# Grouping score and dP chunks by four, with remainder channels at four row positions and the softmax row-sum correction moved out of dS

## The chip, the cores and the metric

The kernel runs on one core of one Trainium2 chip. The metric is the device time of one execution in microseconds (us), as the median of several runs. A core has five engines that run side by side and synchronise by semaphores: PE (matrix multiplies, with PEld for its weight loads), DVE (vector work), ACT (activations, copies with a scale), POOL (general work on the on-chip memory SBUF) and SP (here only a queue that issues transfers). Matmul results go to PSUM, eight banks of accumulation memory, from which DVE and ACT read.

## The reference, cut to what matters

The kernel computes the output and all gradients of one block. B = 2 batches, T = 4000 tokens, D = 144 channels, everything in bfloat16.

```python
xa = _layernorm(x)
qkv = jnp.einsum('btd,de->bte', xa, w_qkv)
scores = jnp.einsum('btd,bsd->bts', q, k) * D ** (-0.5)
p = _softmax(scores, axis=-1)
attn = jnp.einsum('bts,bsd->btd', p, v)
glob = jnp.einsum('btd,de->bte', attn, w_att_out)
...
h = _gelu(jnp.einsum('btd,de->bte', xc, w_mlp_in))
...
m = jnp.concatenate([glob, loc], axis=-1)
...
return x + jnp.einsum('btc,cd->btd', m, w_merge)
...
_out, _vjp = jax.vjp(_f, x, w_qkv, w_att_out, w_mlp_in, dw_csgu, w_mlp_out, dw_merge, w_merge)
_grads = _vjp(grad_out)
```

The part that matters here is attention, forwards and backwards. Per query row the kernel needs P = exp(S - max) unnormalised, its row sum l, Y = P xa / l, then dP (the gradient that reaches P), delta = the row's dot product of Y with dP's own query-side factor, and dS = P (dP - delta) / l. From dS come Z = dS xa (the gradient on the query side) and X, the sum over query rows of dS and P times query-side factors (the gradient on the key and value side).

## The kernel before

The 4000 tokens of a batch are 32 tiles (NB) of 125 tokens (PB). The channels are 128 main ones and 16 remainder ones (DR): `xaT_m` holds the transposed main channels, `R` holds in rows 0 to 15 the remainder channels and in rows 16 to 111 a stack of gradient remainders for other products. Keys are cut into 8 chunks (NG) of 500 (CH).

Each batch runs `phase_att`, then a merge phase; a final phase follows the second batch. `phase_att` is a software pipeline over steps t = 0 to 32. Within a step t the slots s = 0 to 7 hold:

- s = 0 to 3: `S_pair(t, s)`, scores of tile t against two chunks. For each chunk one matmul over the main channels (L683) and one over `R` (L684, 128 rows high, with zero weights beyond the 16). One `ps` tile (two PSUM banks, two such tiles exist in `ps_sg`) takes both chunks. DVE copies the negative to `Pbuf` while it takes the running minimum (L688, L690), ACT writes the exponential over it (L691).
- s = 0: transposes of Z of tile t-3. s = 1: `jit_mm(t + 1)`, the query-side factors `qb`. s = 4: `jit_tr(t + 1)`, their transposes `qt`, the weights of the score and dP matmuls.
- s = 2, 3: `Y_half(t - 1, ...)`, 32 matmuls of 145 columns over the transposed P (`PT`), then on DVE the reciprocal `rl` of the row sum (column 144) and `delta`; on ACT the stored `yn` and `QBs`, both query-side factors times `rl` in one instruction (L725). s = 3 ends with `rescale(t)`, which brings the four quarters of P to one maximum and issues the transposing transfer to `PT` (L703).
- s = 4 to 7: `dP_pair(t - 1, ...)`, which mirrors `S_pair` (L733, L734). DVE makes `Sbuf` = (dP - delta) P from it, one instruction for each chunk (L739).
- s = 6, 7: `Z_half(t - 2, ...)`, 32 matmuls of 144 columns over the transposed dS (`ST`), then ACT's scaled copy `zn`.
- `x(n)`: groups of `X_group`, which multiply `Sbuf` and `Pbuf` blocks of tiles t-3 and t-2 with `QBs` (L794), and DVE's sum into `acc` (L800).
- `local(...)`: units of the other branch of the block (convolution, GELU and their gradients), spread over the steps.

At the end of a step the transposing transfer from `Sbuf` to `ST` is issued (L859). After the loop `last_tr` transposes the last tile's dS on PE, into `PT`, which is free then; the last Z and X follow, mixed with matmuls of the merge phase (`M.fill`). Transfers are issued in order on SP's queue: `Yn_d`, `Zn_d`, `PT`, `ST` and `ug_d`, each behind the one before it. The order on each engine is that of the text, changed in places by a scheduler that orders ready work.

## Time and profile before

| what | us |
|---|---|
| median of 3 runs (lowest to highest) | 1480.2 (1479.16 to 1481.11) |
| the profiled execution, its time | 1477.11 |
| its span, first to last instruction | 1475.3 |
| busy: PE | 1377.6 |
| busy: DVE | 1217.1 |
| busy: ACT | 849.7 |
| busy: POOL | 282.0 |

The profile records one execution. Busy time of an engine is the union of its instructions' times. A line of a group names the source line, engine, operation, the tile written and those read, the shape, how often it occurs, its busy time and the mean ns of one, and the idle time of the engine just before. A duration of PE contains the draining of the array, so that neighbours overlap; the distance between starts says what one costs. The two attention loops lie from 59 to about 655 us and from 770 to about 1365 us of the span.

### The profile page before, as it was taken

How to read it: one execution, taken by the hardware profiler on the slowest of the kernel's cores; microseconds unless marked ns; L12 is line 12 of the kernel's file. 1: busy time of each engine (PE TensorE's matmuls, PEld its weight loads, DVE VectorE, ACT ScalarE, POOL GpSimd, SP SyncE). 2: the span in 40 equal slices, each digit the busy share in tenths (PEclk: the TensorE clock that was granted, in tenths of full speed). 3: DMA queues.
4: the chain of work that ended last, by engine and by line, in shares of the span. 5: the costliest groups of instructions: out<-in, count | busy, mean ns of one | idle time of the engine just before them, and what ended most of it. 6: DMA issues, size and time to landing. Idle time of an engine off the chain costs nothing. (4 is left out here: it accounts for less than half of the span.)

```text
span 1475.3 us, 39163 instructions
## 1 busy us (share of the span) xinstructions
PE 1377.6 (93%) x16184; PEld 1181.5 (80%) x16184; DVE 1217.1 (82%) x3060; ACT 849.7 (58%) x1538; POOL 282.0 (19%) x494
## 2 busy tenths in 40 slices
PE   2789999999999999997888999999999999999898
PEld 1568888888888888887885888888888888888797
DVE  6699888988898988887638998889898889888754
...
GB/s 101 31 144 121 121 121 122 120 122 117 118 115 113 119 118 111 107 138 209 62 56 104 138 122 113 111 121 124 119 123 121 121 121 121 116 117 124 218 35 64
DMA packets 559360, 170.44 MB, mean 116 GB/s; under 512 B 542443, under 2 KB 554093, under 8 KB 559136
## 3 DMA queue, kind: packets, MB, share of 16 engines
...
## 5 line engine op out<-in xcount | busy, mean ns | idle before, releaser
L739 DVE SCALAR_TENSOR_TENSOR Sbuf<-ps,delta,Pbuf 125x500 bf16<-125x500 f32 x512 | 356.0, 731 | 28.2 <-PE ps L734 25.4
L794 PE MATMUL X<-QBs,Sbuf 125*125 125x144 bf16 x2048 | 303.1, 226 | 6.7 <-DVE acc L800 3.0
L794 PE MATMUL X<-QBs,Pbuf 125*125 125x144 bf16 x2048 | 302.1, 226 | 0.0
L794 PEld LDWEIGHTS <-Pbuf 125*125 125x125 bf16 x2048 | 262.1, 137 | 14.9 <-issue 10.3
L794 PEld LDWEIGHTS <-Sbuf 125*125 125x125 bf16 x2048 | 261.9, 137 | 7.7 <-DVE Sbuf L739 2.0
L800 DVE TENSOR_TENSOR acc<-X,acc 125x432 f32<-125x432 f32 x372 | 203.4, 550 | 33.0 <-PE X L794 31.9
L683 PE MATMUL ps<-xaT_m,qt 128*125 128x500 bf16 x512 | 194.6, 380 | 11.2 <-ACT Pbuf L691 9.9
L733 PE MATMUL ps<-xaT_m,qt 128*125 128x500 bf16 x512 | 192.7, 376 | 8.0 <-ACT Pbuf L691 5.7
L684 PE MATMUL ps<-R,qt 128*125 128x500 bf16 x512 | 194.0, 379 | 0.0
L734 PE MATMUL ps<-R,qt 128*125 128x500 bf16 x512 | 191.2, 373 | 0.0
L711 PEld LDWEIGHTS <-PT 125*125 125x125 bf16 x2048 | 147.9, 137 | 24.3 <-DMA PT<-Pbuf 6.5
L755 PEld LDWEIGHTS <-ST 125*125 125x125 bf16 x1984 | 144.2, 138 | 18.1 <-DMA ST<-Sbuf 0.6
L711 PE MATMUL yz<-xa_aug,PT 125*125 125x145 bf16 x2048 | 151.1, 227 | 4.1 <-DMA PT<-Pbuf 4.0
L755 PE MATMUL yz<-xa_aug,ST 125*125 125x144 bf16 x1984 | 147.8, 228 | 0.4 <-DMA ST<-Sbuf 0.4
L684 PEld LDWEIGHTS <-qt 128*125 128x125 bf16 x512 | 70.8, 138 | 33.3 <-issue 14.2
L734 PEld LDWEIGHTS <-qt 128*125 128x125 bf16 x512 | 69.8, 136 | 27.7 <-issue 8.2
L547 POOL TENSOR_TENSOR A_dwc<-l_fl,A_dwc 128x512 f32<-128x512 f32 (+2 forms) x48 | 35.7, 744 | 292.8 <-ACT l_fl L546 292.8
L688 DVE TENSOR_SCALAR_CACHE_REDUCE Pbuf<-ps 125x1000 bf16<-125x1000 f32 x64 | 76.6, 1197 | 14.5 <-PE ps L684 14.3
L733 PEld LDWEIGHTS <-qt 128*125 128x125 bf16 x512 | 70.0, 137 | 23.1 <-DVE Sbuf L739 2.7
L683 PEld LDWEIGHTS <-qt 128*125 128x125 bf16 x512 | 70.6, 138 | 21.9 <-issue 1.3
L759 ACT ACTIVATE zn<-yz,rl 125x144 bf16<-125x144 f32 x64 | 24.2, 378 | 108.5 <-PE yz L755 108.5
L417 POOL TENSOR_SCALAR l_a<-l_sq 125x576 bf16<-125x576 bf16 x32 | 21.4, 670 | 292.6 <-ACT l_sq L415 252.9
...
## 6 DMA issues: line engine op xcount, KB each, us to landing
...
PT<-Pbuf SPq DMA_TRANSPOSE x64
```

The source lines that it names most:

```text
L547: nc.gpsimd.tensor_tensor(acc, fl[0:rows, 0:n], acc, op=ALU.add)
L683: nc.tensor.matmul(ps[:, h, 0:CH], qt[:, 0, :], xaTm[:, cs], start=True, stop=False)
L684: nc.tensor.matmul(ps[:, h, 0:CH], qt[:, 1, :], R[:, cs], start=False, stop=True)
L688: nc.vector.tensor_scalar(pdst, src, -1.0, None, op0=ALU.mult, op1=ALU.min, accum_out=nm[:, 0:1])
L711: nc.tensor.matmul(Y, PT[0:PB, j, 0:PB], xaa[:, j, 0:D + 1], start=(j == 0), stop=(j == NB - 1))
L733: nc.tensor.matmul(ps[:, h, 0:CH], qt[:, 2, :], xaTm[:, cs], start=True, stop=False)
L734: nc.tensor.matmul(ps[:, h, 0:CH], qt[:, 3, :], R[:, cs], start=False, stop=True)
L739: nc.vector.scalar_tensor_tensor(sdst, ps[:, h, 0:CH].rearrange("p (a b) -> p a b", b=PB), DL[i][:], psrc, op0=ALU.subtract, op1=ALU.mult)
L755: nc.tensor.matmul(Z, ST[0:PB, j, 0:PB], xaa[:, j, 0:D], start=(j == 0), stop=(j == NB - 1))
L759: nc.scalar.activation(zn[:, 0:D], Z, ACT.Copy, scale=RL.pop(i)[:])
L794: nc.tensor.matmul(X[:, jj, :], l, r, start=(n_ == 0), stop=(n_ == len(ops) - 1))
L800: nc.vector.tensor_tensor(av, X[:, 0:nj, :], av, op=ALU.add)
```

## The change

- `quad` takes four pieces of work and gives each its own bank: four main matmuls (L684 of the new file), then four remainder matmuls of 16 rows (L688) that are kept behind the last main one. The r-th remainder stands at rows 32r to 32r+15.
- For that, `XR` holds the 16 remainder rows at four row positions, copied out of `R` by four transfers for each two chunks; in `qb` POOL copies the remainder channels to three more places, so that the transposed `qt` has them at the four row positions.
- In a step with both tiles, `products(c2)` groups two score chunks of tile t and two dP chunks of tile t-1. Such a group takes both `ps` tiles.
- `PdP` makes `Sbuf` = dP P, without delta, one DVE instruction for both chunks. The term delta P is put elsewhere: Z gets `ty`, which is -delta / l times Y's unnormalised sum, added (`zs` on ACT, the sum on POOL), and the factor that X multiplies with `Pbuf` gets -delta times the other query-side factor (`nd` and `gq` on POOL). `QBs` is written by two ACT instructions.
- `Y_half(t - 1)` moves to the step's end, `Z_half(t - 2)` behind the second group; the transfer to `ST` is cut in two, the first half behind the second group, the second at the step's end, ahead of `rescale(t)`.
- Behind the loop `last_tr` writes to `ST`; the last tile's Y stands there too, with `late_y` behind it.

```diff
@@ -346,6 +346,10 @@
             for bi in range(8):
                 nc.tensor.transpose(pr[0:DR, bi, 0:PB], S.xa_aug[:, 8 * g + bi, 128:D], W.ident[0:PB, 0:PB])
             nc.vector.tensor_copy(v8(S.R, 8 * g, 8)[0:DR], pr[0:DR, :, 0:PB])
+
+            for r in range(4):
+                c = 2 * g + r % 2
+                nc.sync.dma_start(S.XR[32 * r:32 * r + DR, g, :], S.R[0:DR, c * CH:(c + 1) * CH])
 
         def go_rem():
             nc.gpsimd.tensor_copy(S.go_r[:], go_q[:, :, 128:D])
@@ -641,8 +645,8 @@
             nc.gpsimd.memset(t_[:, :, D:256], 0.0)
         for t_ in znr:
             nc.gpsimd.memset(t_[:, D:256], 0.0)
-        xaTm, R, xaa = S.xaT_m, S.R, S.xa_aug
-        QT, QB, RL, DL, YZ, ZN, ZT, NM, DHT = {}, {}, {}, {}, {}, {}, {}, {}, {}
+        xaTm, R, XR, xaa = S.xaT_m, S.R, S.XR, S.xa_aug
+        QT, QB, RL, TY, YZ, ZN, ZT, NM, DHT = {}, {}, {}, {}, {}, {}, {}, {}, {}
         units = local_units(k, W, b, S, A, es_loc, DHT, ps_w)
 
         def jit_mm(i):
@@ -655,6 +659,8 @@
                 nc.tensor.matmul(pj[:, D:2 * D], S.goT[:, h * PB:(h + 1) * PB], W.VUT[:, kk, 0:D], start=False, stop=(kk == 4))
             qb = qbr[i % 3]
             nc.scalar.copy(qb[:, :, 0:D], pj[:].rearrange("p (a b) -> p a b", b=D))
+            rem_ = qb[:, :, 128:256].rearrange("p a (r c) -> p a r c", c=32)[:, :, :, 0:DR]
+            nc.gpsimd.tensor_copy(rem_[:, :, 1:4, :], rem_[:, :, 0:1, :].to_broadcast([PB, 2, 3, DR]))
             QB[i] = qb
 
         def jit_tr(i):
@@ -670,25 +676,42 @@
         def pchunk(pb, c2):
             return Pbuf[0:PB, pb, c2 * 1024:(c2 + 1) * 1024]
 
-        def S_pair(i, c2):
-            qt = QT[i]
+        def quad(work):
+
+
+            pp = [ps_sg.tile([PB, 2, 512], F32, tag="sg", name="ps") for _ in range(len(work) // 2)]
+            for r, (qt, q, c) in enumerate(work):
+                mm = nc.tensor.matmul(pp[r // 2][:, r % 2, 0:CH], qt[:, q, :], xaTm[:, c * CH:(c + 1) * CH], start=True, stop=False)
+            with tc.issue_after(mm.ins), tc.high_priority():
+                for r, (qt, q, c) in enumerate(work):
+                    rs = slice(32 * r, 32 * r + DR)
+                    nc.tensor.matmul(pp[r // 2][:, r % 2, 0:CH], qt[rs, q + 1, :], XR[rs, c // 2, :], start=False, stop=True)
+            return [p[:, :, 0:CH].rearrange("p h (a b) -> p h a b", b=PB) for p in pp]
+
+        def S_work(i, c2):
+            return [(QT[i], 0, 2 * c2), (QT[i], 0, 2 * c2 + 1)]
+
+        def dP_work(i, c2):
+            return [(QT[i], 2, 2 * c2), (QT[i], 2, 2 * c2 + 1)]
+
+        def pv(buf, n, c2):
+            return buf[0:PB, n, c2 * 1024:(c2 + 1) * 1024].rearrange("p (h a b) -> p h a b", h=2, b=128)[:, :, :, 0:PB]
+
+        def S_exp(i, c2, src):
             if c2 == 0:
                 nm_ = small.tile([PB, 8], F32, tag="nm")
                 NM[i] = nm_
             nm = NM[i]
-            ps = ps_sg.tile([PB, 2, 512], F32, tag="sg")
-            for h in range(2):
-                c = 2 * c2 + h
-                cs = slice(c * CH, (c + 1) * CH)
-                nc.tensor.matmul(ps[:, h, 0:CH], qt[:, 0, :], xaTm[:, cs], start=True, stop=False)
-                nc.tensor.matmul(ps[:, h, 0:CH], qt[:, 1, :], R[:, cs], start=False, stop=True)
-            src = ps[:, :, 0:CH].rearrange("p h (a b) -> p h a b", b=PB)
-            pdst = pchunk(i % NPB, c2).rearrange("p (h a b) -> p h a b", h=2, b=128)[:, :, :, 0:PB]
+            pdst = pv(Pbuf, i % NPB, c2)
             if c2 == 0:
                 nc.vector.tensor_scalar(pdst, src, -1.0, None, op0=ALU.mult, op1=ALU.min, accum_out=nm[:, 0:1])
             else:
                 nc.vector.tensor_scalar(pdst, src, -1.0, nm[:, c2 - 1:c2], op0=ALU.mult, op1=ALU.min, accum_out=nm[:, c2:c2 + 1])
             nc.scalar.activation(pdst, src, ACT.Exp, bias=nm[:, c2:c2 + 1], scale=1.0)
+
+        def PdP(i, c2, src):
+
+            nc.vector.tensor_tensor(pv(Sbuf, i % NDB, c2), src, pv(Pbuf, i % NPB, c2), op=ALU.mult)
 
         def rescale(i):
             nm = NM.pop(i)
@@ -703,7 +726,7 @@
             nc.sync.dma_start_transpose(out=PT[:], in_=Pbuf[:, i % NPB, :])
 
         def Y_half(i, h):
-            if h == 0:
+            if h == 0 and i not in YZ:
                 yz = ps_yz.tile([PB, 2, 145], F32, tag="yz")
                 YZ[i] = yz
             Y = YZ[i][:, 0, :]
@@ -716,27 +739,22 @@
             RL[i] = rl
             nc.vector.reciprocal(rl[:], Y[:, 144:145])
             delta = small.tile([PB, 1], F32, tag="delta")
-            DL[i] = delta
             dj = small.tile([PB, D], BF, tag="dj", bufs=1)
             nc.vector.scalar_tensor_tensor(dj[:], Y[:, 0:D], rl[:], qb[:, 1, 0:D], op0=ALU.mult, op1=ALU.mult, accum_out=delta[:])
             yn = small.tile([PB, D], BF, tag="yn", bufs=2)
             nc.scalar.activation(yn[:], Y[:, 0:D], ACT.Copy, scale=rl[:])
             nc.sync.dma_start(S.Yn_d[:, i, :], yn[:])
-            nc.scalar.activation(QBs[:, i % NPB], qb[:, :, 0:D], ACT.Copy, scale=rl[:])
-
-        def dP_pair(i, c2):
-            qt = QT[i]
-            ps = ps_sg.tile([PB, 2, 512], F32, tag="sg")
-            for h in range(2):
-                c = 2 * c2 + h
-                cs = slice(c * CH, (c + 1) * CH)
-                nc.tensor.matmul(ps[:, h, 0:CH], qt[:, 2, :], xaTm[:, cs], start=True, stop=False)
-                nc.tensor.matmul(ps[:, h, 0:CH], qt[:, 3, :], R[:, cs], start=False, stop=True)
-            for h in range(2):
-                c = 2 * c2 + h
-                psrc = Pbuf[0:PB, i % NPB, c * 512:(c + 1) * 512].rearrange("p (a b) -> p a b", b=128)[:, :, 0:PB]
-                sdst = Sbuf[0:PB, i % NDB, c * 512:(c + 1) * 512].rearrange("p (a b) -> p a b", b=128)[:, :, 0:PB]
-                nc.vector.scalar_tensor_tensor(sdst, ps[:, h, 0:CH].rearrange("p (a b) -> p a b", b=PB), DL[i][:], psrc, op0=ALU.subtract, op1=ALU.mult)
+            nd = small.tile([PB, 2], F32, tag="nd")
+            nc.gpsimd.tensor_scalar(nd[:, 0:1], delta[:], -1.0, None, op0=ALU.mult)
+            nc.gpsimd.tensor_tensor(nd[:, 1:2], nd[:, 0:1], rl[:], op=ALU.mult)
+            gq = small.tile([PB, D], F32, tag="gq", bufs=1)
+            nc.gpsimd.tensor_scalar(gq[:], qb[:, 0, 0:D], nd[:, 0:1], None, op0=ALU.mult)
+            nc.gpsimd.tensor_tensor(gq[:], gq[:], qb[:, 1, 0:D], op=ALU.add)
+            ty = small.tile([PB, D], F32, tag="ty", bufs=2)
+            nc.scalar.activation(ty[:], Y[:, 0:D], ACT.Copy, scale=nd[:, 1:2])
+            TY[i] = ty
+            nc.scalar.activation(QBs[:, i % NPB, 0, :], qb[:, 0, 0:D], ACT.Copy, scale=rl[:])
+            nc.scalar.activation(QBs[:, i % NPB, 1, :], gq[:], ACT.Copy, scale=rl[:])
 
         def last_tr(c2):
 
@@ -744,9 +762,9 @@
             sb = Sbuf[0:PB, (NB - 1) % NDB, c2 * 1024:(c2 + 1) * 1024].rearrange("p (a b) -> p a b", b=128)
             for j in range(8):
                 nc.tensor.transpose(pt[0:PB, j, 0:PB], sb[:, j, 0:PB], W.ident[0:PB, 0:PB])
-            (nc.vector.tensor_copy if c2 % 2 else nc.scalar.copy)(PT[0:PB, 8 * c2:8 * c2 + 8, 0:PB], pt[0:PB, :, 0:PB])
-
-        def Z_half(i, h, ST=ST):
+            (nc.vector.tensor_copy if c2 % 2 else nc.scalar.copy)(ST[0:PB, 8 * c2:8 * c2 + 8, 0:PB], pt[0:PB, :, 0:PB])
+
+        def Z_half(i, h):
             if h == 0 and i + 1 not in YZ:
                 yz = ps_yz.tile([PB, 2, 145], F32, tag="yz")
                 YZ[i + 1] = yz
@@ -756,7 +774,9 @@
             if h == 0:
                 return
             zn = znr[i % 2]
-            nc.scalar.activation(zn[:, 0:D], Z, ACT.Copy, scale=RL.pop(i)[:])
+            zs = small.tile([PB, D], F32, tag="zs", bufs=1)
+            nc.scalar.activation(zs[:], Z, ACT.Copy, scale=RL.pop(i)[:])
+            nc.gpsimd.tensor_tensor(zn[:, 0:D], zs[:], TY.pop(i)[:], op=ALU.add)
             nc.sync.dma_start(S.Zn_d[:, i, :], zn[:, 0:D])
             ZN[i] = zn
 
@@ -823,40 +843,51 @@
                 for _ in range(n):
                     if xg:
                         X_group(*xg.pop(0))
-            for s in range(8):
-                if s < 4 and ok(t):
-                    S_pair(t, s)
-                if s >= 4 and ok(t - 1):
-                    dP_pair(t - 1, s - 4)
-                if t == NB and s == 4:
-                    M.late_y()
-                if s == 0:
-                    if ok(t - 3):
-                        zt_tr(t - 3)
-                    x(1)
-                elif s == 1:
-                    if ok(t + 1):
-                        jit_mm(t + 1)
-                    x(1)
-                elif s in (2, 3):
+            def loc(f):
+                local(-(-int(n_units * (t + f) * 1000) // (1000 * (NB - 1))))
+
+            def products(c2):
+                if t < NB:
+                    ps = quad((S_work(t, c2) if ok(t) else []) + (dP_work(t - 1, c2) if ok(t - 1) else []))
+                    S_exp(t, c2, ps[0])
                     if ok(t - 1):
-                        Y_half(t - 1, s - 2)
-                    if s == 3 and ok(t):
-                        rescale(t)
-                elif s == 4:
-                    if ok(t + 1):
-                        jit_tr(t + 1)
-                    x(1)
-                elif s == 5:
-                    x(1)
-                else:
-                    if ok(t - 2) and t < NB:
-                        Z_half(t - 2, s - 6)
-                    x(1)
-                local(-(-n_units * (8 * t + s + 1) // (8 * (NB - 1))))
+                        PdP(t - 1, c2, ps[1])
+                elif c2 < 2:
+                    for q, src in enumerate(quad(dP_work(t - 1, 2 * c2) + dP_work(t - 1, 2 * c2 + 1))):
+                        PdP(t - 1, 2 * c2 + q, src)
+            products(0)
+            if ok(t - 3):
+                zt_tr(t - 3)
+            loc(0.25)
+            if ok(t + 1):
+                jit_mm(t + 1)
+            loc(0.5)
+            x(1)
+            products(1)
+            for h in range(2):
+                if ok(t - 2):
+                    Z_half(t - 2, h)
+            if ok(t - 1) and t < NB:
+                nc.sync.dma_start_transpose(out=ST[:, 0:NB // 2, :], in_=Sbuf[:, (t - 1) % NDB, 0:GW // 2])
+            x(1)
+            loc(0.6)
+            products(2)
+            if ok(t + 1):
+                jit_tr(t + 1)
+            x(1)
+            loc(0.95)
+            x(1)
+            products(3)
+            if t < NB:
+                for h in range(2):
+                    if ok(t - 1):
+                        Y_half(t - 1, h)
+            loc(1.0)
             x(6)
-            if t < NB and ok(t - 1):
-                nc.sync.dma_start_transpose(out=ST[:], in_=Sbuf[:, (t - 1) % NDB, :])
+            if t < NB:
+                if ok(t - 1):
+                    nc.sync.dma_start_transpose(out=ST[:, NB // 2:NB, :], in_=Sbuf[:, (t - 1) % NDB, GW // 2:GW])
+                rescale(t)
             if t == NB - 1:
                 M.open_early(ST)
         es_sg.close()
@@ -865,17 +896,17 @@
         xg = X_groups(NB + 1)
         for c2 in range(4):
             last_tr(c2)
+        zt_tr(NB - 2)
+        for h in range(2):
+            Y_half(NB - 1, h)
+        M.late_y()
+        M.fill(2)
+        for h in range(2):
+            Z_half(NB - 1, h)
+        for _ in range(5):
             X_group(*xg.pop(0))
-        Z_half(NB - 2, 0)
-        Z_half(NB - 2, 1)
+        M.fill(4)
         X_group(*xg.pop(0))
-        M.fill(2)
-        Z_half(NB - 1, 0, PT)
-        Z_half(NB - 1, 1, PT)
-        zt_tr(NB - 2)
-        M.fill(2)
-        X_group(*xg.pop(0))
-        M.fill(2)
         zt_tr(NB - 1)
         for g_ in X_groups(NB + 2):
             X_group(*g_)
@@ -1291,6 +1322,7 @@
     bx = pool(ctx, "bx", "left")
     xaT_m = bx.tile([128, T], BF, name="xaT_m")
     R = bx.tile([128, T], BF, name="R")
+    XR = bx.tile([128, G8, CH], BF, name="XR")
     go_r = bx.tile([PB, NB + 6, DR], BF, name="go_r")
     goT = bx.tile([128, (NB + 4) * PB], BF, name="goT")
     acc = bx.tile([PB, NB, D], F32, name="acc")
@@ -1300,7 +1332,7 @@
     SS = [K() for _ in range(B)]
     SS[0].xa_aug = px0.tile([PB, NB, XW], BF, name="xa_aug0")
     for b, S in enumerate(SS):
-        S.xaT_m, S.R, S.go_r, S.goT, S.acc, S.rstd_x = xaT_m, R, go_r, goT, acc, rstd[b]
+        S.xaT_m, S.R, S.XR, S.go_r, S.goT, S.acc, S.rstd_x = xaT_m, R, XR, go_r, goT, acc, rstd[b]
         for nm in ("Yn", "ug", "Zn"):
             setattr(S, nm + "_d", tc.dram_tile([PB, NB, D], BF, name="%s_d%d" % (nm, b)))
     A = K()
```

## The prediction

> **What bounds the kernel now.** I read the page's totals first, then its groups.
>
> ```profile
> PE 1377.6 (93%) x16184; PEld 1181.5 (80%) x16184; DVE 1217.1 (82%) x3060; ACT 849.7 (58%) x1538; POOL 282.0 (19%) x494
> ...
> L739 DVE SCALAR_TENSOR_TENSOR Sbuf<-ps,delta,Pbuf 125x500 bf16<-125x500 f32 x512 | 356.0, 731 | 28.2 <-PE ps L734 25.4
> ...
> L684 PE MATMUL ps<-R,qt 128*125 128x500 bf16 x512 | 194.0, 379 | 0.0
> ...
> L688 DVE TENSOR_SCALAR_CACHE_REDUCE Pbuf<-ps 125x1000 bf16<-125x1000 f32 x64 | 76.6, 1197 | 14.5 <-PE ps L684 14.3
> ```
>
> PE leads, with DVE not far behind. An average hides stages, so next comes a stretch of 24 whole steps of the first attention loop, cut at first score matmuls.
>
> ```profile
> core 0: us, PE busy (x) PEld busy (x) DVE busy (x) ACT busy (x) POOL busy (x), PEclk, DMA share, GB/s
> 137.57:592.45 454.88, 446.49 (x5188) 382.08 (x5187) 403.42 (x939) 283.02 (x510) 53.36 (x84) 1.00 0.66 118
> ```
>
> Divided by 24, a step takes 18.95 us: PE is busy 18.60, DVE 16.81, ACT 11.79, POOL 2.22, at a full clock. PE sets the step and idles 0.35 us of it. The second loop's stretch has the same 446.5 in 454.7. What a matmul costs is not its 380 ns (they overlap) but the distance to the next start, from PE's order of time:
>
> ```profile
> 306.95 0.37 PE L683 MATMUL ps<-xaT_m,qt 128*125 128x500 bf16 x1
> 307.16 0.37 PE L684 MATMUL ps<-R,qt 128*125 128x500 bf16 x1
> 307.37 0.37 PE L683 MATMUL ps<-xaT_m,qt 128*125 128x500 bf16 x1
> 307.58 0.37 PE L684 MATMUL ps<-R,qt 128*125 128x500 bf16 x1
> 307.79 0.27 PE L767 MATMUL pt<-ident,zn 125*128 125x125 bf16 x2
> ```
>
> Four take 0.84 us: 211 ns each, and the remainder (L684, 16 useful rows) as much as the main part. Eight such pairs make 6.75 us of a step. Matmuls of 144 columns, Y, Z and X, follow each other at 63 ns (twelve of X from 307.90 to 308.66).
>
> **What PE saves.** The change replaces, per four chunks, eight full-height matmuls (8 x 211 = 1688 ns) by four mains (844) and four 16-row remainders at four row positions. No row of this trace shows matmuls side by side at different row positions. If all four run together they cost one, 211 ns; if none do, 844. Between stands the weight load: loads of 125 columns follow each other at 58 ns in the stream of L514 (five in 0.45 us, each 0.22 long), so I let the four start 58 ns apart: 211 + 3 x 58 = 385. The nearest end is the lower one, since each has its own weights, rows and bank; I do not take it because every remainder still needs its load.
>
> Changing between 128 and 16 rows is in the trace, in the preparation:
>
> ```profile
> 41.46 0.22 PE L231 MATMUL pt<-ident,Wi 128*96 128x128 bf16 x1
> 41.61 0.20 PE L232 MATMUL pt<-ident,Wi 16*96 16x16 bf16 x1
> 41.75 0.26 PE L231 MATMUL pt<-ident,Wi 128*96 128x128 bf16 x1
> 41.93 0.20 PE L232 MATMUL pt<-ident,Wi 16*96 16x16 bf16 x1
> 42.07 0.26 PE L231 MATMUL pt<-ident,Wi 128*96 128x128 bf16 x1
> ```
>
> There and back takes 0.32 us (41.75 to 42.07). Streaming explains 55 ns for 128 columns (L480) and at most as much for 16, so the two changes cost 210 to 265 ns. Changing to 80 rows (L1054) shows no such pause; if this one belonged to the transposes alone the price would be zero. Same rows, same engine: I take 250 ns for the there and back of a group.
>
> A group then costs 844 + 385 + 250 = 1479 ns and saves 209; four groups save 0.84 us a step. The ends: 844 + 211 + 0 = 1055 saves 2.53 us a step, and 844 + 844 + 265 = 1953 loses 1.06.
>
> The Trainium skill, "TensorE: Matmul & The Clock Gate", section "Part 3: Packing small matmuls — row/col tiling", gives 3.07x for four row tiles of 512 columns. By that figure an estimate of the remainders is 844 / 3.07 = 275 ns, a group 1369, and the total below would come to 1404; no row here shows it.
>
> **What the other engines get.** DVE: eight STTs of 731 ns become four tensor-tensor products over 1000 elements. L800 takes 298 ns for 144 and 600 for 432 elements, 1.05 ns an element: 1196 for 1000, as L688's 1197. DVE falls by 5.85 - 4.78 = 1.06 us to 15.75 a step; not counted in the sum, since PE stays above it.
>
> ACT: one 288-column scaling of 532 (L725) becomes two of about 378 (L759's size), and ty adds one: 0.6 us, to 12.4. POOL: six small operations a step. By L547's 80x144 sum (485), L338 (561 upper, 471 lower for L338's first batch), L459 (272) and L925 (180) they are 2 x 180 + 470 + 2 x 485 + 272 = 2.1 us, to 4.3 of 18. Neither engine is near the step. In the loops DVE's L739 takes 731 ns on average where POOL is idle (398 cases) and 735 where POOL works beside it (54), so more POOL work costs DVE nothing.
>
> The added wait is on ACT: ty waits for nd, the second QBs scaling for gq, both on POOL. Behind them stand the rescale and the next step's first exponential. Y's end, reciprocal 0.17, dot 0.45, POOL 1.3, hops 0.4, scalings 0.4: 2.7 us, then rescale 1.4. The next first exponential is wanted after 21 matmuls of X (1.3), a group (1.5) and the minimum (1.3): 4.1. It fits exactly. A 1.29 us POOL sum (L547) in between makes it late by that much, and PE's next group late with it; that falls in about one step of four, 0.1 us a step on the sum below as a cost.
>
> SP: the transfer of ST is cut in two; a whole one occupies the queue as follows.
>
> ```profile
> L859 SPq DMA_TRANSPOSE ST<-Sbuf x62: 4764/4855/6453, 87.3 to 1362.3; - x62
> ```
>
> The second half, behind yn's store, is issued about 1.2 us after Y's end and (half of 4.9, plus half of the whole's 5 us of traffic, partly overlapped) is there about 5 us after it. Z's second half starts 7.6 us after (X 1.3, group 1.5, fill 2.5, group 1.5, first Z half 1.0, less the overlap). 2 us of cover; PT has a whole step. If the cover went, PE would wait and DVE after it. The 16 XR copies per batch are 0.25 us each on SP, behind R's copies and past the stores of the merge; only a step's last group needs the last of them. I take 0.5 us a batch (0 to 3).
>
> **Score buffers.** A group takes both ps buffers, where a pair took one. The next group waits for minimum, exponential and product.
>
> ```profile
> 308.40 1.19 DVE L688 TENSOR_SCALAR_CACHE_REDUCE Pbuf<-ps 125x1000 bf16<-125x1000 f32 x1
> ...
> 309.63 1.10 ACT L691 ACTIVATE Pbuf<-ps,nm__4762 125x1000 bf16<-125x1000 f32 x1 [1.17 <-DVE Pbuf L688]
> ```
>
> That is 1.2 to 1.3 + 1.1 + hops: 2.6 us. PE's other work of a step, 18.60 - 6.75 = 11.85 us, lies in four stretches: by the order of the program, about 2.5 (jit, local), 3.0 (Z and X), 2.6 and 3.6 (Y and X). So the wait is just covered if DVE starts the minimum at once; DVE's work per stretch is about 4.3, 3.2, 4.3 and 4.6 us against PE's 4.0, 4.5, 4.1 and 5.1, so it catches up. I raise idle time from 0.35 to 0.45 us, the 0.1 from ACT's wait.
>
> **The sum.** A step: 18.60 - 0.84 + 0.45 = 18.21, 0.74 less than 18.95; 62 steps (31 a loop) give -46. Half groups at each loop's first step cost 4 x 2 x 0.1 = +0.8. The tail, with Y of the last tile behind the transposes, is between -2 and +4 a batch, +1 taken, since POOL's loads have 19 us between Yn's store (656) and its reading (682); XR +1. The profiled execution took 1477.1 us by its timing (span 1475.3 and 1.8 around it): 1477.1 - 46 + 4 = 1435. The median of the runs, 1480.2, lies 3 above: 1438.
>
> **Rivals.**
>
> Remainders start together and the change of rows costs its least: group 844 + 211 + 210 = 1265, saving 1.69 us a step, PE at 16.9, DVE at 15.75 next to bind; with 0.4 idle, 17.3 a step, -102: 1382. For it: nothing in the four shares rows or a bank; against: the loads. With free changes of rows PE and DVE meet near 16 and it reaches 1335.
>
> The wait for both buffers decides (slower): DVE is 87% busy, and an X sum of 0.6 us (L800) queued before a minimum delays the buffers by that. The forecast's margin is 0.74 us a step, 0.19 a group; above that the kernel is slower. With half the groups delayed 0.6 and 0.05 of hops, 0.35 a group or 1.4 a step: +0.66 x 62 = +41, 1521. For it: before, the wait of DVE's minimum for PE was 51.9 us in 70 cases (the list of waits) and PE's for the exponential 9.9 in 13, with a spare buffer, now gone; against: the stretches above. The Trainium skill, "TensorEngine Tiling (Array Packing)", "PSUM Bottleneck", warns of this: evacuation may bind after tiling.
>
> The remainders don't run side by side, so the change does not do what it says: 1.0 us a step more, +62: 1545. For it: not one row shows them together.
>
> Gain and waits cancel: about 1478.
>
> **Chances.** Forecast (1405 to 1465 for its own terms) 0.45; start together 0.22; buffers 0.13; not side by side 0.12; cancel 0.08 (faster 0.03, same 0.04, slower 0.01). Faster by over 0.2%, about what a measurement here tells from nothing: 0.45 + 0.22 + 0.03 = 0.70; same 0.04; slower 0.13 + 0.12 + 0.01 = 0.26. The range 1365 to 1525 leaves out the case that they don't run side by side (0.12) and, of the first two rivals, what lies beyond it (0.08).
>
> **What would show it.** In PE's order of time the four remainders start 58 ns apart (4 or fewer: first rival; 211: third), with 0.1 us pauses before and after. The product row reads near 1196 x 256. DVE falls to about 1150 us. PE's waits for ACT's exponential and DVE's product stay under 0.45 us a step; much more, and the second rival holds. Gaps of PE before Z for ST, or of ACT for nd and gq over 1 us, would prove my covers wrong.

## The result, and the profile after

| | us |
|---|---|
| before, median of 4 (beside these runs) | 1479.68 |
| the change, median of 4 (1542.91 to 1545.45) | 1543.96 |
| ratio, 95% interval | 1.0434 [1.0416, 1.0452] |
| span of the profiled execution, before and after | 1475.3 and 1543.2 |

The kernel became 4.3% slower, outside the range of the prediction and on the other side of no change. The totals and groups of its page (busy time, mean of one, idle time before and what ended it):

```profile
PE 1322.6 (86%) x16184; PEld 1078.5 (70%) x16184; DVE 1178.0 (76%) x2804; ACT 888.0 (58%) x1666; POOL 440.9 (29%) x878
...
L684 PE MATMUL ps<-xaT_m,qt 128*125 128x500 bf16 x1024 | 276.9, 382 | 38.8 <-ACT Pbuf L710 34.9
L714 DVE TENSOR_TENSOR Sbuf<-ps,Pbuf 125x1000 bf16<-125x1000 f32 x256 | 305.8, 1196 | 1.8 <-issue 1.4
...
L734 PE MATMUL yz<-xa_aug,PT 125*125 125x145 bf16 x2048 | 153.6, 233 | 31.0 <-DMA PT<-Pbuf 31.0
```

PE and DVE are both busy for less time than before (1377.6 and 1217.1), and the kernel is longer: the work shrank as intended and idle time took its place. The new idle time stands in the right part of the rows: mains wait for ACT's exponential, Y for PT. Twenty-four whole steps of the first loop, in the view of windows:

```profile
core 0: us, PE busy (x) PEld busy (x) DVE busy (x) ACT busy (x) POOL busy (x), PEclk, DMA share, GB/s
...
146.20:612.20 466.00, 420.90 (x5178) 340.17 (x5177) 386.85 (x840) 297.64 (x560) 112.19 (x229) 1.00 0.65 115
```

Divided by 24: a step takes 19.42 us against 18.95, PE is busy 17.54 of them against 18.60, so it idles 1.88 where it idled 0.35. What the remainders became is in PE's order of time:

```profile
543.74 1.01 PE L684 MATMUL ps<-xaT_m,qt 128*125 128x500 bf16 x4 [0.38 <-ACT Pbuf L710]
544.68 0.43 PE L688 MATMUL ps<-XR,qt 16*125 16x500 bf16 x4
545.04 0.34 PE L671 MATMUL pt<-ident,qb 125*128 125x125 bf16 x3
```

From the first main to the next other matmul a group of four chunks takes 1.30 us; eight full-height matmuls took 1.69. The trace's separate starts of the four remainders lie within 10 ns in the 77 groups of this stretch that it shows whole, some 3 ns apart: they run side by side.

The waits of the whole span (total, times, longest):

```profile
ACT QBs L757 <- POOL gq L752: 43.6, 62, 1.3
...
PE ps L684 <- ACT Pbuf L710: 34.9, 70, 1.6
...
PE yz L734 <- DMA PT<-Pbuf: 31.0, 8, 13.9
...
PE X L814 <- ACT zt L789: 8.1, 14, 1.4
```

ACT waits for gq in 62 of the 64 tiles, 0.70 us each. What it waits for, at the end of one step, first on POOL and then on ACT:

```profile
515.81 0.23 POOL L748 TENSOR_SCALAR nd<-delta 125x1 f32<-125x1 f32 x1 [5.18 <-DVE dj L743]
516.12 0.25 POOL L749 TENSOR_TENSOR nd<-nd,rl 125x1 f32<-125x1 f32 x1
516.36 0.65 POOL L751 TENSOR_SCALAR gq<-qb,nd 125x144 f32<-125x144 bf16 x1
517.09 0.46 POOL L752 TENSOR_TENSOR gq<-gq,qb 125x144 f32<-125x144 f32 x1
```

```profile
516.45 0.37 ACT L754 ACTIVATE ty<-yz,nd 125x144 f32<-125x144 f32 x1
517.58 0.42 ACT L757 ACTIVATE QBs<-gq,rl 125x144 bf16<-125x144 f32 x1 [0.76 <-POOL gq L752]
517.89 0.35 ACT L789 COPY zt<-pt 128x250 bf16<-128x250 bf16 x1
```

From the dot product's start (515.35) to the second half of QBs (518.0) the chain is 2.65 us long, 1.74 of it on POOL, and the copy of zt (the transposes of Z), which PE needs, stands behind it. That is how the wait reaches PE: in the 54 steady steps of the table below PE waits for zt 44 times, 30.3 us in all (the last row above is one of several), and without the chain 4 times, 3.9 us (no_chain, below).

To see which stage pays, each trace is cut at the start of DVE's first minimum of tiles 0, 4 and 31 in both batches: start, first four steps, 27 further steps, middle (from tile 31 of the first batch to tile 0 of the second), end. Lengths in us, loops added up; the last column is the time in the loops' first four steps with PE's clock granted at half.

| | span | start | first four, both loops | 54 steady steps | middle | end | half clock, first four |
|---|---|---|---|---|---|---|---|
| before | 1475.3 | 61.5 | 119.1 | 1028.9 | 137.6 | 128.2 | 10.8 |
| the change | 1543.2 | 59.2 | 137.9 | 1054.7 | 147.9 | 143.6 | 39.6 |
| difference | +67.9 | -2.3 | +18.8 | +25.8 | +10.3 | +15.4 | |

In the steady steps PE is busy for 955.0 us where it was 1010.6, and idle for 99.7 where it was 18.4.

### The profile page after: what moved, and what is told of

Same layout as the page of the kernel before. It is cut to its first block, busy times and chain, and to the rows that moved or that the text cites. A ratio compares the mean times of both kernels' runs of the same rounds, so it can differ in the third digit from the quotient of the medians.

```text
span 1543.2 us, 39555 instructions
## 1 busy us (share of the span) xinstructions
PE 1322.6 (86%) x16184; PEld 1078.5 (70%) x16184; DVE 1178.0 (76%) x2804; ACT 888.0 (58%) x1666; POOL 440.9 (29%) x878
## 4 chain that ended last, share of the span: by engine, by line
PE 31%; DVE 27%; ACT 15%; POOL 12%; issue 8%; DMA 7%; DVEq 0%; SPq 0%; POOLq 0%; ACTq 0%
DVE Pbuf L709 8%; PE ps L684 7%; ACT Pbuf L710 7%; PE X L814 5%; DVE Sbuf L714 5%; DMA PT<-Pbuf 4%; PE yz L773 4%; PE ps L688 3%; DVE acc L820 3%; PE po L1083 2%; POOL gq L751 2%; PE yz L734 2%; DVE Pbuf L723 1%; POOL gq L752 1%; POOL nd L748 1%
## 5 line engine op out<-in xcount | busy, mean ns | idle before, releaser
L684 PE MATMUL ps<-xaT_m,qt 128*125 128x500 bf16 x1024 | 276.9, 382 | 38.8 <-ACT Pbuf L710 34.9
L714 DVE TENSOR_TENSOR Sbuf<-ps,Pbuf 125x1000 bf16<-125x1000 f32 x256 | 305.8, 1196 | 1.8 <-issue 1.4
L814 PEld LDWEIGHTS <-Pbuf 125*125 125x125 bf16 x2048 | 261.6, 137 | 33.6 <-issue 32.8
L814 PEld LDWEIGHTS <-Sbuf 125*125 125x125 bf16 x2048 | 261.7, 137 | 13.5 <-issue 12.7
L684 PEld LDWEIGHTS <-qt 128*125 128x125 bf16 x1024 | 129.1, 139 | 78.1 <-issue 44.2
L773 PEld LDWEIGHTS <-ST 125*125 125x125 bf16 x2048 | 141.2, 140 | 18.8 <-issue 14.7
L688 PE MATMUL ps<-XR,qt 16*125 16x500 bf16 x1024 | 114.1, 426 | 0.0
L688 PEld LDWEIGHTS <-qt 16*125 16x125 bf16 x1024 | 36.1, 129 | 99.7 <-issue 99.7
L725 ACT ACTIVATE Pbuf<-Pbuf,f 125x1000 bf16<-125x1000 bf16 x64 | 72.3, 1129 | 1.5
L673 ACT COPY qt<-pt 128x500 bf16<-128x500 bf16 x64 | 36.6, 571 | 61.8 <-PE pt L671 61.8
L723 DVE TENSOR_SCALAR Pbuf<-Pbuf,f 125x1000 bf16<-125x1000 bf16 x128 | 60.6, 488 | 10.9 <-ACT f L719 10.9
L1083 PE MATMUL po<-VUl,YT 128*125 128x144 bf16 x640 | 54.1, 231 | 4.4 <-ACT goT L307 4.4
L1004 PE MATMUL Hps<-Yg,go_h 125*128 125x144 bf16 x640 | 55.2, 232 | 2.8 <-DMA Yg<-ug_d 2.0
```

The costliest lines, as they stand in the source:

```text
L684: mm = nc.tensor.matmul(pp[r // 2][:, r % 2, 0:CH], qt[:, q, :], xaTm[:, c * CH:(c + 1) * CH], start=True, stop=False)
L688: nc.tensor.matmul(pp[r // 2][:, r % 2, 0:CH], qt[rs, q + 1, :], XR[rs, c // 2, :], start=False, stop=True)
L714: nc.vector.tensor_tensor(pv(Sbuf, i % NDB, c2), src, pv(Pbuf, i % NPB, c2), op=ALU.mult)
L723: nc.vector.tensor_scalar(pdst, pdst, f[:, c2:c2 + 1], None, op0=ALU.mult)
L773: nc.tensor.matmul(Z, ST[0:PB, j, 0:PB], xaa[:, j, 0:D], start=(j == 0), stop=(j == NB - 1))
L814: nc.tensor.matmul(X[:, jj, :], l, r, start=(n_ == 0), stop=(n_ == len(ops) - 1))
```

## Experiments: the parts alone

Theory: the chain of small operations on POOL, which ACT waits for, costs what PE saves and more. Rivals: the wait for two buffers at a time; the new order; the row positions themselves. The first four kernels cut the change along these lines.

**delta_only.** Before, with the softmax correction moved, and nothing else (the code is the change's; pairs of full height, the order and the whole ST transfer stay):

```diff
-            nc.scalar.activation(QBs[:, i % NPB], qb[:, :, 0:D], ACT.Copy, scale=rl[:])
+            nc.gpsimd.tensor_scalar(nd[:, 0:1], delta[:], -1.0, None, op0=ALU.mult)
+            nc.gpsimd.tensor_tensor(nd[:, 1:2], nd[:, 0:1], rl[:], op=ALU.mult)
+            nc.gpsimd.tensor_scalar(gq[:], qb[:, 0, 0:D], nd[:, 0:1], None, op0=ALU.mult)
+            nc.gpsimd.tensor_tensor(gq[:], gq[:], qb[:, 1, 0:D], op=ALU.add)
...
-                nc.vector.scalar_tensor_tensor(sdst, ps[:, h, 0:CH]..., DL[i][:], psrc, op0=ALU.subtract, op1=ALU.mult)
+            nc.vector.tensor_tensor(pv(Sbuf, i % NDB), src, pv(Pbuf, i % NPB), op=ALU.mult)
```

> The kernel before with one part of the change alone: delta taken out of dS and put on Z and on the query side (nd, gq, ty on POOL and ACT, one product of 1000 elements on DVE); order, pairs and full-height remainders as before. Theory 'buffers' (a group that takes both score buffers makes the engines wait for each other): within 1% of before, 1470 to 1490, since DVE only loses 1.06 us a step off the path. Theory 'chain' (ACT stands behind POOL's nd and gq): 0.7 us a step and the tails slower, 1510 to 1530.

**order_spread.** The change with single pairs of full height, spread over the step:

```diff
-            products(0)
+            sc(0)
...
+            dp(0)
...
-            products(1)
+            sc(1)
...
+            dp(1)
```

> The change with its new order, its delta and its halved ST transfers, but scores and dP in single pairs with other work between them, remainders full height as before. PE's work is back at 18.6 us a step. Theory 'buffers': the waits go with the groups, 18.9 us a step plus the longer tails, 1485 to 1510. Theory 'order' (the moved Y and Z and the new spread of local units cost the time): 1535 or more, no better than the change.

**group_full_height.** The change, groups and all, but its remainders read all 128 rows. As in order_spread, the XR transfers and POOL's copies of the remainder channels (0.26 us each in the median) are gone too:

```diff
-                    rs = slice(32 * r, 32 * r + DR)
-                    nc.tensor.matmul(pp[r // 2][:, r % 2, 0:CH], qt[rs, q + 1, :], XR[rs, c // 2, :], start=False, stop=True)
+                    nc.tensor.matmul(pp[r // 2][:, r % 2, 0:CH], qt[:, q + 1, :], R[:, c * CH:(c + 1) * CH], start=False, stop=True)
```

> The change with its groups of four, but the remainders full height as before, not at row positions. Theory that PE's own work still sets the step: each group costs 1.69 instead of 1.30 us, 1.55 us a step more, about 1640. Theory that waits between engines set it: only part of that, 1560 to 1600. If the row positions themselves cost time: below 1544.

**no_chain.** The change without nd, gq, ty, zs and POOL's sum, so that its gradients lack the term delta P:

```diff
-            nc.scalar.activation(QBs[:, i % NPB, 0, :], qb[:, 0, 0:D], ACT.Copy, scale=rl[:])
-            nc.scalar.activation(QBs[:, i % NPB, 1, :], gq[:], ACT.Copy, scale=rl[:])
+            nc.scalar.activation(QBs[:, i % NPB], qb[:, :, 0:D], ACT.Copy, scale=rl[:])
...
-            nc.gpsimd.tensor_tensor(zn[:, 0:D], zs[:], TY.pop(i)[:], op=ALU.add)
+            nc.scalar.activation(zn[:, 0:D], Z, ACT.Copy, scale=RL.pop(i)[:])
```

> The change without the correction by delta: nd, gq, ty, zs and the sum into zn are left out, QBs is one instruction again, so ACT never waits for POOL. Theory 'chain': 0.7 us a step and about 20 us at the two tails come back, 1475 to 1490. Theory 'buffers': the tails alone, 1520 to 1535.

| | median, us | ratio to before | first four | steady | middle | end |
|---|---|---|---|---|---|---|
| delta_only | 1523.18 | 1.0301 [1.0284, 1.0319] | 124.3 | 1052.6 | 147.0 | 136.9 |
| order_spread | 1521.74 | 1.0281 [1.0266, 1.0296] | 122.3 | 1054.8 | 148.8 | 135.5 |
| group_full_height | 1557.43 | 1.0521 [1.05, 1.0542] | 136.6 | 1070.5 | 148.4 | 139.4 |
| no_chain | 1490.95 | 1.0075 [1.0052, 1.0097] | 136.4 | 1024.1 | 134.4 | 135.2 |

Moving the correction alone, in the kernel before, costs 43.6 us against the 1479.62 measured beside it; taking it out of the change gives back 53. The new order is worth next to nothing (1.4 us, order_spread against delta_only). Groups cost: 35.7 us from order_spread to group_full_height, 14.3 of them in the first four steps, where no X, Z or Y of earlier tiles lies between two groups, and 15.7 in the steady ones. Row positions give 13.5 back (the change against group_full_height): in the steady steps they spare PE 67.4 us of busy time, and 51.5 of it return as idle time (48.2 to 99.7). So the chain is the largest cost, and groups and row positions nearly cancel in the steady steps. The first theory holds that far. It does not say whether ACT's wait is the price or something else in the chain.

## Experiments: what of the chain costs

**chain_on_pool, delta_pool.** The whole chain on POOL: ty is made from yn, POOL scales the second half of QBs, and ACT waits for none of it. The same edit goes into the change (chain_on_pool) and into delta_only, that is with pairs (delta_pool):

```diff
+            nc.gpsimd.tensor_scalar(QBs[:, i % NPB, 1, :], gq[:], rl[:], None, op0=ALU.mult)
...
-            nc.scalar.activation(ty[:], Y[:, 0:D], ACT.Copy, scale=nd[:, 1:2])
+            nc.gpsimd.tensor_scalar(ty[:], yn[:], nd[:], None, op0=ALU.mult)
...
-            nc.scalar.activation(QBs[:, i % NPB, 1, :], gq[:], ACT.Copy, scale=rl[:])
```

> The whole change with the same chain on POOL alone. Theory 'ACT behind POOL': the loops fall to those of no_chain, 581 us each, the tails stay 15 us long in all: 1505 to 1515. Else it stays at 1540.

> The kernel before with delta moved as in delta_only, but the chain wholly on POOL: ty is made from the stored yn, the second half of QBs is scaled by POOL, so ACT issues nothing that waits for POOL there. POOL's work grows by two operations a tile. Theory 'ACT behind POOL': the loops return to before's 574 us each, 1480 to 1495, the rest being POOL's queue at the two tails. Theory that the added work itself (ACT 0.6, POOL 2 us a step) costs the time: 1515 or more.

**tail_on_dve, exp_from_sbuf.** To chain_on_pool: the last tile's chain and the last two sums of zn on DVE, and Y ahead of the fourth group in the last step (tail_on_dve). To that, the exponential from the negated scores in SBUF, which are rounded to bf16, so that the minimum alone holds ps (exp_from_sbuf):

```diff
+            e_ = nc.vector if i == NB - 1 else nc.gpsimd
...
-            nc.gpsimd.tensor_tensor(zn[:, 0:D], zs[:], TY.pop(i)[:], op=ALU.add)
+            (nc.vector if i >= NB - 2 else nc.gpsimd).tensor_tensor(zn[:, 0:D], zs[:], TY.pop(i)[:], op=ALU.add)
```

```diff
-            nc.scalar.activation(pdst, src, ACT.Exp, bias=nm[:, c2:c2 + 1], scale=1.0)
+            nc.scalar.activation(pdst, pdst, ACT.Exp, bias=nm[:, c2:c2 + 1], scale=-1.0)
```

> As chain_on_pool, with the last tile's chain and the last two sums into zn on DVE, and in the loop's last step Y ahead of the fourth group, so that the last transfer to PT can start earlier. Theory that POOL's queue and PT's transfer make the tails longer: 15 to 20 us less than chain_on_pool, 1485 to 1495. If the tails have another cause: no change.

> As tail_on_dve, and ACT takes the exponential from the negated bfloat16 scores that DVE has just written to Pbuf, not from ps, so that a group's first score buffer is free 1.1 us earlier (the scores are rounded to bfloat16 first). Theory 'buffers': PE's 1.0 us a step of waits for ACT's exponential and DVE's product shrinks by about half, 20 to 40 us less than tail_on_dve, 1450 to 1475. If the waits for the buffers only stand in for ACT's and DVE's queues: under 10 us.

| | median, us | ratio to before | first four | steady | middle | end |
|---|---|---|---|---|---|---|
| delta_pool | 1498.58 | 1.0137 [1.0113, 1.0161] | 126.9 | 1027.3 | 148.1 | 133.8 |
| chain_on_pool | 1545.55 | 1.0459 [1.0433, 1.0485] | 137.6 | 1048.5 | 151.5 | 149.5 |
| tail_on_dve | 1523.18 | 1.0308 [1.0269, 1.0348] | 136.6 | 1047.2 | 147.3 | 130.0 |
| exp_from_sbuf | 1509.51 | 1.0218 [1.0194, 1.0241] | 131.2 | 1038.5 | 148.9 | 132.8 |

With pairs, ACT's part in the chain was the whole steady price: without its wait (25.5 us in the whole span of delta_only) and its two scalings, 1052.6 falls to 1027.3, before's length. With groups the same edit brings 6 us (1054.7 to 1048.5), and 24 above no_chain's stay. PE's wait for zt falls with it, from 30.3 to 10.6 us of the steady steps, but other waits take its place: 7.5 us for the half of QBs that POOL now writes, and 9.7 more for DVE's product. In the whole span of chain_on_pool:

```profile
PE X L813 <- POOL QBs L753: 25.9, 24, 3.0
```

With groups, then, ACT's wait is not the whole price; the edit moves the end of the chain from ACT to POOL. In the tail the last sum and the last chain stand in POOL's queue, as the change's order of time shows it in the middle stretch:

```profile
674.97 0.18 POOL L956 COPY gate<-ST 1x1 bf16<-1x1 bf16 x1
675.10 0.54 POOL L958 DMA_DIRECT2D go_h<-in_grad_out_dram  x1
...
695.70 0.49 POOL L779 TENSOR_TENSOR zn<-zs,ty 125x144 bf16<-125x144 f32 x1
696.17 0.24 POOL L748 TENSOR_SCALAR nd<-delta 125x1 f32<-125x1 f32 x1
```

The last tiles' sum and chain stand behind 20 us of loads. Off POOL and with Y earlier, middle and end fall by 24 us (301.0 to 277.3). But only 4.2 of that is in the middle. The end has 19.5, and there chain_on_pool shows one long wait of PE:

```profile
1445.75 0.38 PE L734 MATMUL yz<-xa_aug,PT 125*125 125x145 bf16 x1 [19.68 <-DMA PT<-Pbuf]
```

In tail_on_dve the longest wait for PT is 4.1 us. So the gain goes with the late PT more than with POOL's queue, and no run separates the two edits.

**y_third.** An attempt to start the chain earlier: Y behind the third group, Z behind the fourth, the ST transfer whole at the step's end.

```diff
-                nc.sync.dma_start_transpose(out=ST[:, NB // 2:NB, :], in_=Sbuf[:, (t - 1) % NDB, GW // 2:GW])
                 rescale(t)
+                nc.sync.dma_start_transpose(out=ST[:], in_=Sbuf[:, (t - 1) % NDB, :])
```

> As exp_from_sbuf, with Y behind the third group instead of the fourth and Z behind the fourth, the transfer to ST whole at the step's end. The chain from Y to the factors of X has then a group and a Z more before the next step's X wants them. Theory 'chain at the step's end': the 54 steady steps fall by 15 to 25 us in all, 1480 to 1495. If the chain's place does not matter: 1505 to 1515. Below 1479 it would beat both kernels.

It took 1661.47 us, 1.1229 [1.1201, 1.1257], and tells nothing of the chain: with Y wanted sooner, PT comes too late in nearly every step. From its waits:

```profile
PE yz L734 <- DMA PT<-Pbuf: 132.8, 54, 4.9
```

## Experiments: the bound, and POOL's queue

**no_chain_exp, no_chain_exp_full.** no_chain with the exponential from SBUF, and the same with remainders of full height; the edits are those shown above.

> The change without the correction by delta (as no_chain), and with the exponential taken from Pbuf (as exp_from_sbuf), so that neither the chain nor the late release of the first score buffer is there. Theory that chain and buffers are what ate PE's gain: 1465 to 1478, below no_chain by 13 or more and below before. If something else holds the steps: within 6 us of no_chain.

> As no_chain_exp, with the remainders full height again: PE has 1.55 us a step, some 98 us, more to do. Theory that waits between engines, not PE's work, set the step with groups: 20 to 45 us above no_chain_exp. Theory that PE's work binds once the chain is gone: 70 us or more above.

**pool_load.** no_chain_exp, with POOL's chain put back so that nobody reads what it makes:

```diff
+            nc.gpsimd.tensor_scalar(gq[:], qb[:, 0, 0:D], nd[:], None, op0=ALU.mult)
+            nc.gpsimd.tensor_tensor(gq[:], gq[:], qb[:, 1, 0:D], op=ALU.add)
+            gs = small.tile([PB, D], BF, tag="gs", bufs=1)
+            nc.gpsimd.tensor_scalar(gs[:], gq[:], rl[:], None, op0=ALU.mult)
+            nc.gpsimd.tensor_scalar(ty[:], yn[:], nd[:], None, op0=ALU.mult)
+            nc.gpsimd.tensor_tensor(gs[:], ty[:], gq[:], op=ALU.add)
```

> no_chain_exp with POOL doing the chain's operations all the same, into tiles that nobody reads: POOL is as occupied as in the change with its chain, and nothing waits for it. The correction by delta is left out of the result, as in no_chain_exp. Theory 'the dependency costs' (ACT and X's factors late): within 8 us of no_chain_exp's 1464. Theory 'POOL's time costs' (its operations for the local units and its transfers come late): 1480 or more.

**stt_chain.** exp_from_sbuf with the chain off POOL but for ty:

```diff
+            nc.vector.scalar_tensor_tensor(gq[:], qb[:, 0, 0:D], nd[:], qb[:, 1, 0:D], op0=ALU.mult, op1=ALU.add)
+            nc.scalar.activation(QBs[:, i % NPB, 1, :], gq[:], ACT.Copy, scale=rl[:])
...
+            nc.vector.scalar_tensor_tensor(zn[:, 0:D], Z, RL.pop(i)[:], TY.pop(i)[:], op0=ALU.mult, op1=ALU.subtract)
```

> exp_from_sbuf with a shorter chain at the end of a step: nd and gq on DVE (gq in one instruction with two operations), ACT scales gq into QBs[1] at once, ty on POOL where nobody waits for it soon, and the sum of Z in one DVE instruction instead of zs, zn and POOL's sum. Nothing is left out. Theory 'the chain's length from Y to X's factors is what still costs': the 54 steady steps fall from exp_from_sbuf's 1038 us to within 10 us of no_chain_exp's 1012, and the time to 1465-1485, level with before or a little below. DVE gains some 0.7 us a step (16.1 to 16.8, under a step of 18.7). Theory 'grouping itself (matmuls that wait for the buffers) is what still costs': it stays at 1500-1515.

| | median, us | ratio to before | first four | steady | middle | end |
|---|---|---|---|---|---|---|
| no_chain_exp | 1464.11 | 0.9904 [0.9884, 0.9923] | 124.7 | 1012.5 | 132.0 | 134.4 |
| no_chain_exp_full | 1492.6 | 1.0095 [1.0079, 1.0112] | 124.0 | 1045.3 | 133.5 | 126.9 |
| pool_load | 1490.55 | 1.0071 [1.0051, 1.0092] | 124.4 | 1035.9 | 137.2 | 129.7 |
| stt_chain | 1482.32 | 1.0014 [0.9997, 1.0032] | 121.1 | 1023.0 | 147.1 | 128.5 |

With nothing waiting for the chain, pool_load still loses 23.4 us in the steady steps, where exp_from_sbuf stands 26.0 above no_chain_exp. POOL's occupancy alone is enough for nearly the whole price. That the dependency costs nothing does not follow: in exp_from_sbuf's steady steps PE waits 9.3 us for POOL's half of QBs, and pool_load's block on POOL is longer at this place by one sum (0.49 us). Which steps pay, first loop, us per step:

```
tile           7    8    9   10   11   12   22   23   24   25   26
no_chain_exp 22.3 17.1 18.8 18.9 19.5 17.0 20.1 17.9 19.2 16.7 20.2
pool_load    24.5 18.7 18.8 18.9 20.8 17.1 22.4 18.6 20.8 17.7 20.4
```

Seven steps (7, 8, 11, 22 to 25) hold 10.9 of the 11.0 us by which the loop's 27 steady steps differ; every other step agrees to 0.4. The same seven hold 10.8 of the 12.9 us of exp_from_sbuf, whose chain is read. The end of tile 7's step in pool_load, one engine at a time. POOL:

```profile
194.79 0.22 POOL L749 TENSOR_SCALAR nd<-delta 125x1 f32<-125x1 f32 x1 [3.86 <-DVE dj L743]
195.12 0.72 POOL L751 TENSOR_SCALAR gq<-qb,nd 125x144 f32<-125x144 bf16 x1
...
197.83 0.49 POOL L757 TENSOR_TENSOR gs<-ty,gq 125x144 bf16<-125x144 f32 x1
198.28 0.72 POOL L440 TENSOR_TENSOR rsr<-ve,mhalf 125x2 f32<-125x2 f32 x1
```

DVE, ACT and PE behind it:

```profile
199.03 0.16 DVE L456 SCALAR_TENSOR_TENSOR rsr<-mv,rsr 125x2 f32<-125x2 f32 x1 [2.85 <-POOL rsr L440]
```

```profile
199.23 0.90 ACT L458 ACTIVATE gd<-l_hg,rsr 125x144 bf16<-125x144 bf16 x2 [3.47 <-DVE rsr L456]
200.04 0.34 ACT L787 COPY zt<-pt 128x250 bf16<-128x250 bf16 x1
```

```profile
200.44 0.28 PE L516 MATMUL pd<-dgs,gS 80*125 80x145 bf16 x1 [3.68 <-ACT zt L787]
```

L440 is a power over 250 numbers for a local unit's normalisation. It was ready when DVE had made ve (195.98), but stood behind the chain until 198.28. DVE waited for it, ACT for DVE, and the copy of zt behind ACT, so PE stood still for 3.68 us for an operand that has nothing to do with either. In no_chain_exp the same place on POOL, then ACT, then PE:

```profile
193.50 0.71 POOL L440 TENSOR_TENSOR rsr<-ve,mhalf 125x2 f32<-125x2 f32 x1 [5.12 <-DVE ve L439]
```

```profile
194.44 0.90 ACT L458 ACTIVATE gd<-l_hg,rsr 125x144 bf16<-125x144 bf16 x2 [1.24 <-DVE rsr L456]
```

```profile
195.64 0.22 PE L516 MATMUL pd<-dgs,gS 80*125 80x145 bf16 x1 [1.45 <-ACT zt L777]
```

PE waits for 1.45 us there instead of 3.68, and the step is as much shorter (22.3 for 24.5).

The Trainium skill, "TensorE: Matmul & The Clock Gate", section "Architectural detail: the array is 16× 32×32, not 1× 128×128", says that ACT and DVE take their work strictly first in, first out, and GpSimd so on each of its Q7 cores. The rows above agree, with 2.30 us for L440; the prediction did not apply it to what stands behind the chain on POOL.

The gap also costs clock. Two windows of pool_load, around it:

```profile
192.00:198.80 6.80, 4.76 (x63) 3.92 (x61) 4.19 (x15) 3.14 (x5) 3.74 (x7) 1.00 0.59 114
198.80:205.60 6.80, 4.91 (x32) 3.66 (x31) 5.61 (x17) 3.77 (x8) 0.64 (x3) 0.50 0.68 129
```

From 198.8, inside the gap (196.76 to 200.44), the granted clock (the third column from the right) stands at 0.50 for 6.8 us, in which PE has 4.91 us of work. In the steady steps of both loops pool_load has 27.3 us at half clock and no_chain_exp none. Of pool_load's 23.4 us, 13.9 are idle time of PE, and 9.5 are longer work on the same matmuls.

stt_chain fits this, in a kernel that leaves nothing out: with ty alone of the chain left on POOL the steady steps fall by 15.5 us (1038.5 to 1023.0) and the time is level with before. It also shortens the chain, so it does not tell occupancy from dependency. Its middle is still long, 14.7 us of it in one wait on PE:

```profile
670.86 0.38 PE L734 MATMUL yz<-xa_aug,PT 125*125 125x145 bf16 x1 [14.71 <-DMA PT<-Pbuf]
```

**stt_gate_pt, stt_gate_ty, before_exp.** Three last kernels: the merge's loads held back until PT has landed; on top of it ty on DVE; and, as a control, before with the exponential from SBUF.

```diff
-        g_ = nc.gpsimd.tensor_copy(gate[:], ST[0:1, NB - 1, 0:1])
+        g_ = nc.gpsimd.tensor_copy(gate[:], PT[0:1, NB - 1, 0:1])
```

```diff
-            (nc.vector if i == NB - 1 else nc.gpsimd).tensor_scalar(ty[:], yn[:], delta[:], None, op0=ALU.mult)
+            nc.vector.tensor_scalar(ty[:], yn[:], delta[:], None, op0=ALU.mult)
```

> stt_chain with one edit: the copy on POOL behind which the loads for the merge are issued reads PT of the last tile instead of ST, so the loads start when PT has landed. In stt_chain PE waited 14.7 us for PT in the middle, the loads being in the DMA engines at the same time; without the chain it waited 2.7. Theory 'the loads delay PT': the middle stretch falls from 147 us to 132-138, and the time to 1466-1473, under before. If the wait only moves to Hps (the loads late): 1478-1486, no gain.

> stt_gate_pt with ty on DVE instead of POOL, so that POOL has nothing of the chain and no operation that waits for the end of Y. Theory 'POOL's queue holds up the local units': some 5-10 us under stt_gate_pt (its 54 steady steps at 1012-1018 against stt_chain's 1023), for 0.3 us of DVE a step. Theory 'POOL with one operation is harmless, DVE's time is what costs now': the same or slower.

> before with one edit: the exponential reads the negated scores in SBUF that the minimum wrote, instead of ps, so ps is free after the minimum. A control for exp_from_sbuf and what builds on it. With pairs there is a spare buffer, and PE waits 0.09 us a step for the exponential: 1470-1480, at most 0.5% faster. If it gains over 15 us, what looked like a gain of the groups in no_chain_exp is the exponential's.

| | median, us | ratio to before | first four | steady | middle | end |
|---|---|---|---|---|---|---|
| stt_gate_pt | 1494.8 | 1.0086 [1.0047, 1.0124] | 124.4 | 1023.4 | 152.4 | 133.0 |
| stt_gate_ty | 1496.15 | 1.0111 [1.0085, 1.0137] | 122.1 | 1029.9 | 148.8 | 131.8 |
| before_exp | 1479.22 | 1.0 [0.9984, 1.0015] | 122.2 | 1026.8 | 137.0 | 129.9 |

Both attempts to better stt_chain failed. With the loads held back, Y still waits 9.9 us for PT, and the merge phase (Hps and what follows) then waits for its loads, Yg: the middle grew by 5.3 us and the end by 4.5. ty on DVE lengthens the steady steps by 6.5: what the move may have won on POOL, DVE's time took back and more. The exponential's edit is worth nothing with pairs, so its gain (13.7 us from tail_on_dve to exp_from_sbuf, 26.8 from no_chain to no_chain_exp) belongs to groups that hold both buffers. No kernel that computes everything was measurably faster than before.

## Why the prediction was wrong

**The step that failed** is the added wait: "It fits exactly", charged with "0.1 us a step", together with "Neither engine is near the step". PE's idle time was to be 0.45 us a step and was 1.88. Three things were wrong. By its own figures, 1.29 us late in one step of four, the charge was 0.32 us a step and not 0.1, some 14 us more over 62 steps. POOL's part of the chain took 1.74 us, not 1.3, so that the exact fit was gone: ACT waited for gq in each of 24 steps of the first loop, 0.72 us on average, and PE for the zt behind it, 30.3 us in the steady steps. With pairs, ACT's part alone cost 25.3 us of steady time (delta_only to delta_pool). And POOL was judged by its share (4.3 of 18 us; 4.67 measured): that an engine is free three quarters of the time says nothing of what is queued behind the chain when it runs. pool_load shows that with groups this alone is enough for 23 us. The text named ACT's queue behind the wait, and of POOL's only the 1.29 us sum ahead of the chain, not L440 behind it. Chain in all: 53 us of the median (no_chain), 30.6 of it in steady steps, 21.9 in middle and end.

**The ends** were put at +1 a batch, from -2 to +4. Middle and end grew by 25.7 us; without the chain by 3.8. I gave POOL's loads 19 us of room (the two times named, 656 and 682, are 26 apart; 19 is the distance from the gate's copy at 662.2) and placed nothing else in that queue; the last sum and the last chain stand in it behind the loads, at 695.7 and 696.2 with the gate at 675.0. In the end, which grew by 15.4, most is Y's late PT: one wait of 13.9 us for it, where before's longest was 1.1. That part is not the chain's alone, since no_chain still waits 9.5 there.

**The first four steps of each loop** were not looked at: +18.8 us. They have little work to put between two groups, so that the wait for both buffers lies open. This belongs to the groups: with full-height remainders these steps are 17.5 us longer than before's (group_full_height), with pairs 3.2 (order_spread). What shortens them is to free the first buffer earlier (136.4 to 124.7, no_chain to no_chain_exp). The half clock (39.6 us for 10.8) goes with PE's gaps but is not the main price: no_chain_exp has 35.0 us of it and is 5.6 longer than before.

**PE's saving** was sized too small and still not received. A group takes 1302 ns in the median against the forecast 1479: the remainders start 3 ns apart, not 58 (the first rival's reading), the pause from main to remainder is 304 - 211 = 93 ns, and the last remainder's start to the next matmul 351 ns. By distances that is 4 x (1.688 - 1.302) = 1.54 us a step, where 0.84 was forecast; PE's busy time, in which the last matmul before a gap counts in full, fell by 1.07. In the change itself the row positions bring 13.5 us (against group_full_height); with chain and exponential out of the way 28.5 (no_chain_exp against no_chain_exp_full, 32.8 in steady steps), of a possible 96 (1.54 x 62). In the steady steps of these two, PE's busy time falls by 69.1 us and its idle time grows by 36.3. The largest part is the wait for DVE's product, which holds the second buffer (20.2 us for 4.1), while DVE is busy 16.08 us of a step of 18.66; the rest was not taken further apart. The Trainium skill, "TensorE: Matmul & The Clock Gate", "Part 3: Packing small matmuls — row/col tiling", gives starts about 4 ns apart; the trace agrees with 3. An estimate by that page's 3.07 times was 275 ns for the remainders; 351 ns were measured from the last one's start to the next matmul, with the switch back in it. With that estimate the prediction's sum gives 1411, not the 1404 that it names.

**Buffers.** "So the wait is just covered" was half right: PE waits 0.54 us a step for the exponential against 0.09 before, above the 0.45 at which I had said that the second rival holds. Its price, 41 us, was net of PE's saving; groups cost 35.7 and row positions returned 13.5, so 22 net were measured, and the chain came on top. The third rival's time, 1545, was hit by accident: its reason, remainders one after another, is refuted.

**Right:** the product at 1196 ns x 256; ACT at 12.4 us a step; the cover of the halved ST transfer (PE waited 2.9 us for ST in all). DVE fell by 39 us in all, not 66: the replaced instructions overlapped (356.0 us busy over 512, 695 ns each, where I took their mean of 731), and 0.69 a step was measured for 1.06.

**Open:** why the same POOL work costs nothing in steady steps with pairs (delta_pool, 1027.3) and 23 us with groups. delta_pool keeps the order of before as well as pairs, so its chain stands in the middle of the step; its PE idles 20.4 us in the steady steps and never falls to half clock there, where pool_load has 81.0 and 27.3. Groups may leave fewer points at which PE can go on with something else, but no run separates groups from order here.
